# Two batches per step, K=192 as 128 plus two concurrent 64-row tiles, x transposed by DMA, and a fixed interleave of two matmul stages

## The chip, the cores and the metric

The kernel runs on one core of one Trainium2 chip. The metric is the device time of one execution in microseconds. Most executions of one kernel agree within 0.3%. Every kernel below was timed beside runs of the kernel before, on the same chip and in the same rounds. One run of all was over 1.5% above the fastest of its kernel and counts as slow; all ratios are between fast runs.

Engine names in the profile: PE is the matmul engine (TensorE), PEld its weight loads, DVE VectorE, ACT ScalarE, POOL GpSimd, SP the engine that issues most DMAs.

## The reference, cut to what matters

```python
def _attn_ref(x, weight):                 # x 8 x 4096 x 192, weight 8 heads x 7 taps
    w = softmax(weight, axis=-1)          # shortened here
    x_pad = concat([zeros(B, 6, D), x], axis=1)
    # out[b, s, head h's 24 columns] = sum over k of w[h, k] * x_pad[b, s + k, ...]

def _moe_ref(x, w_in, w_out, beta):       # x 32768 x 192, w_in 192 x 2048, w_out 2048 x 192
    h = x @ w_in
    g = h * (1.0 / (1.0 + np.exp(-beta * h)))
    return g @ w_out
```

A causal seven-tap filter over the tokens is followed by a two-layer network. Both layers together need, per 512 tokens, 16 blocks of 128 hidden features times K=192, and then K=2048 back to 192 columns.

## The kernel before

It walks through 64 tiles of 512 tokens. For each one, x is loaded with a cast to bf16, transposed on TensorE, copied out of PSUM (the memory that matmuls write to), filtered on VectorE, and multiplied twice. The 192 input features lie on two sets of 96 partitions, so every hidden block takes two matmuls of 96 rows.

```python
        x_bf = xbf_pool.tile([128, N_BLK, D], BF16)
        nc.gpsimd.dma_start(out=x_bf, in_=x_view[st])
        ptr = psum_tr.tile([128, 2 * N_BLK, BLK], BF16)
        for blk in range(N_BLK):
            nc.tensor.transpose(ptr[:DA, blk, :], x_bf[:, blk, 0:DA], ident)
            nc.tensor.transpose(ptr[:DB, N_BLK + blk, :], x_bf[:, blk, DA:D], ident)
        # ... two copies PSUM -> xt_a, xt_b; then 7 taps for a and 7 for b on VectorE -> ct_a, ct_b

        g_t = g_pool.tile([128, NF, ST_TOK], BF16)
        for pair in range(NF // 2):
            ph = psum_h.tile([128, 2, ST_TOK], FP32)
            for i in range(2):
                fc = 2 * pair + i
                nc.tensor.matmul(ph[:, i, :], w_in_sa[:DA, ts(fc, 128)], ct_a[:DA, :],
                                 start=True, stop=False)
                nc.tensor.matmul(ph[:, i, :], w_in_sb[:DB, ts(fc, 128)], ct_b[:DB, :],
                                 start=False, stop=True)
            nc.scalar.activation(g_t[:, 2 * pair : 2 * pair + 2, :], ph, AF.Silu)

        for half in range(N_BLK // 2):
            po = psum_o.tile([128, 2, D], FP32)
            for j in range(2):
                blk = 2 * half + j
                for fc in range(NF):
                    nc.tensor.matmul(po[:, j, :], g_t[:, fc, ts(blk, BLK)], w_out_s[:, fc, :],
                                     start=(fc == 0), stop=(fc == NF - 1))
            nc.vector.tensor_copy(o_sb[:, 2 * half : 2 * half + 2, :], po)
        nc.sync.dma_start(out=out_view[st], in_=o_sb)
```

The order on each engine is left to the scheduler of the framework.

## Time and profile before

| | before |
|---|---|
| median time | 1060.89 us (1060.8 to 1062.44, 3 runs) |
| TensorE busy | 85% |
| share of TensorE in the chain of waits | 78% |
| hidden matmul, start to next start, clock 1.00 | 0.2155 us |
| output matmul, start to next start | 0.0825 to 0.0865 us |
| one 512-token tile without a stall | 13.25 us |

From the page of the kernel before: busy time by engine, and busy tenths in 40 slices of the span (PEclk is the granted TensorE clock).

```profile
PE 902.9 (85%) x6656; PEld 581.1 (55%) x6656; DVE 635.5 (60%) x1313; ACT 503.7 (48%) x516; POOL 49.1 (5%) x70
PE   1699798897979979799797988979799797997968
PEclk9999899898998989899898998989989899998989
```

TensorE is nearly always busy, but with regular dips, and the clock dips with it. The groups of instructions say what the work is; the columns are line, engine, operation, tiles, shape, count, then busy time and mean duration of one, then idle time before them and what ended it.

```profile
L197 ACT ACTIVATE g_t<-ph 128x1024 bf16<-128x1024 f32 x512 | 500.5, 1021 | 540.8 <-PE ph L190 539.6
L183 PE MATMUL ph<-ct_a,w_in_sa 96*128 96x512 bf16 x1024 | 411.9, 402 | 118.7 <-DVE ct_a L171 114.3
L190 PE MATMUL ph<-ct_b,w_in_sb 96*128 96x512 bf16 x1024 | 411.0, 402 | 0.0
L205 PE MATMUL po<-w_out_s,g_t 128*128 128x192 bf16 x4096 | 386.9, 247 | 2.7
```

Durations of matmuls overlap, so a matmul's price, its *slot*, is the distance between two starts and not its mean duration: 0.2155 us, and not 0.402 us. The 114 us on the second line are TensorE waiting for the taps. The view of stretches of time shows the two regimes (columns: stretch in us, its length, busy time and count by engine, clock, DMA share, GB/s).

```profile
503.80:512.50 8.70, 1.23 (x19) 0.99 (x18) 8.70 (x17) 0.00 (x0) 2.30 (x3) 0.81 0.78 113
512.50:516.00 3.50, 3.47 (x9) 1.23 (x9) 3.50 (x11) 1.02 (x1) 0.00 (x0) 0.50 0.01 2
527.10:540.30 13.20, 13.07 (x102) 8.59 (x101) 4.57 (x10) 7.75 (x8) 0.00 (x0) 1.00 0.09 31
```

In the first stretch TensorE does almost nothing (1.23 of 8.70 us, transposes) while VectorE works without a break; in the second it is back, at half clock; in the third it is the limit at full clock.

The two matmul stages alone cost (32 x 0.2155 + 64 x 0.0845) x 64 = 787 us if every slot is full. So 273 of the 1060 us are something else: stalls, half clock, transposes, start and end.

### The profile page before, as it was taken

The page shows a single profiled execution, that of the slowest core. Times are in us where ns is not written, and L with a number is a line of the kernel's source. Part 1 is how long each engine was busy: PE and PEld are TensorE (multiplying, and loading weights), DVE is VectorE, ACT ScalarE, POOL GpSimd, SP SyncE. Part 2 cuts the span into 40 slices and gives each one's busy share as a digit, 9 for nine tenths or more (in the row PEclk, how much of TensorE's full clock was granted, in tenths as well). Part 3 has the DMA queues.
Part 4 walks back from the last instruction along what each step waited for, and adds up shares of the span by engine and source line. Part 5 has one row for each costly group of instructions (what it writes and reads, how often), then busy time and mean ns, then how long its engine had stood idle before and what let it go on. Part 6 is the DMA issues. An engine that isn't in the chain of part 4 may idle for free.

```text
span 1059.0 us, 15609 instructions
## 1 busy us (share of the span) xinstructions
PE 902.9 (85%) x6656; PEld 581.1 (55%) x6656; DVE 635.5 (60%) x1313; ACT 503.7 (48%) x516; POOL 49.1 (5%) x70
## 2 busy tenths in 40 slices
PE   1699798897979979799797988979799797997968
PEld 1366466464655646466464664646556464664645
DVE  5874564847547485464946548475474854649461
ACT  1355364453535535355353644535355352553534
POOL 2000000000000000000000000000000000000000
PEclk9999899898998989899898998989989899998989
DMA  9111312112130121301212121121201213012100
GB/s 208 12 38 38 53 32 42 32 38 38 38 54 15 38 39 38 53 16 38 41 45 44 32 43 31 38 38 38 53 16 38 38 38 53 16 38 39 37 16 31
DMA packets 72438, 42.96 MB, mean 41 GB/s; under 512 B 37232, under 2 KB 72048, under 8 KB 72048
## 3 DMA queue, kind: packets, MB, share of 16 engines
q0 software_dynamic: 33792, 12.59, 10.9%
q1 hardware_dynamic: 38576, 29.38, 8.7%
q8 instruction: 52, 0.85, 0.3%
q14 instruction: 18, 0.15, 0.0%
HBM read 29.37 MB, written 25.17 MB: 52 GB/s over the span
## 4 chain that ended last, share of the span: by engine, by line
PE 78%; DVE 13%; ACT 4%; DMA 2%; issue 1%; SPq 0%; ACTq 0%
PE po L205 33%; PE ph L183 24%; PE ph L190 21%; DVE ct_b L163 5%; DVE ct_a L163 5%; ACT g_t L197 4%; DMA beta_t<-in_moe_beta_dram 2%; DVE o_sb L212 1%; DVE ct_a L171 1%; DVE xt_b L143 1%; DVE xt_a L142 0%; DVE ct_b L159 0%; DVE ct_a L159 0%; DVE w_out_s L123 0%; SPq L78 0%
## 5 line engine op out<-in xcount | busy, mean ns | idle before, releaser
L197 ACT ACTIVATE g_t<-ph 128x1024 bf16<-128x1024 f32 x512 | 500.5, 1021 | 540.8 <-PE ph L190 539.6
L183 PE MATMUL ph<-ct_a,w_in_sa 96*128 96x512 bf16 x1024 | 411.9, 402 | 118.7 <-DVE ct_a L171 114.3
L190 PE MATMUL ph<-ct_b,w_in_sb 96*128 96x512 bf16 x1024 | 411.0, 402 | 0.0
L205 PE MATMUL po<-w_out_s,g_t 128*128 128x192 bf16 x4096 | 386.9, 247 | 2.7
L205 PEld LDWEIGHTS <-g_t 128*128 128x128 bf16 x4096 | 343.1, 98 | 71.0 <-ACT g_t L197 17.1
L212 DVE COPY o_sb<-po 128x384 f32<-128x384 f32 x128 | 71.1, 556 | 381.2 <-PE po L205 381.2
L163 DVE SCALAR_TENSOR_TENSOR ct_b<-xt_b,cw_b,ct_b 96x512 bf16<-96x512 bf16 x320 | 236.7, 740 | 0.0
L163 DVE SCALAR_TENSOR_TENSOR ct_a<-xt_a,cw_a,ct_a 96x512 bf16<-96x512 bf16 x320 | 236.6, 739 | 0.0
L190 PEld LDWEIGHTS <-w_in_sb 96*128 96x128 bf16 x1024 | 103.6, 101 | 233.2 <-issue 158.5
L183 PEld LDWEIGHTS <-w_in_sa 96*128 96x128 bf16 x1024 | 103.5, 101 | 125.8 <-issue 34.1
L133 POOL DMA_DIRECT2D x_bf<-in_x_dram x64 | 48.5, 760 | 905.1 <-PE ptr L138 903.9
L137 PE MATMUL ptr<-ident,x_bf 128*96 128x128 bf16 x256 | 39.1, 226 | 30.5 <-DMA x_bf<-in_x_dram 15.6
L137 PEld LDWEIGHTS <-x_bf 128*96 128x96 bf16 x256 | 31.0, 127 | 39.1 <-issue 17.5
L142 DVE COPY xt_a<-ptr 96x512 bf16<-96x512 bf16 x64 | 26.5, 413 | 22.4 <-PE ptr L138 22.4
L138 PE MATMUL ptr<-ident,x_bf 128*96 128x128 bf16 x256 | 38.6, 224 | 0.0
L138 PEld LDWEIGHTS <-x_bf 128*96 128x96 bf16 x256 | 31.0, 128 | 4.4
L171 DVE TENSOR_TENSOR ct_b<-xt_b,ct_b 96x512 bf16<-96x512 bf16 x64 | 26.5, 413 | 0.0
L171 DVE TENSOR_TENSOR ct_a<-xt_a,ct_a 96x512 bf16<-96x512 bf16 x64 | 26.4, 412 | 0.0
L143 DVE COPY xt_b<-ptr 96x512 bf16<-96x512 bf16 x64 | 26.2, 410 | 0.0
L159 DVE TENSOR_SCALAR ct_a<-xt_a,cw_a 96x512 bf16<-96x512 bf16 x64 | 23.0, 360 | 0.0
L159 DVE TENSOR_SCALAR ct_b<-xt_b,cw_b 96x512 bf16<-96x512 bf16 x64 | 21.8, 340 | 0.0
L150 DVE COPY xt_b<-xt_b 96x6 bf16<-96x6 bf16 x56 | 9.0, 160 | 0.0
(30 smaller groups left out, 25.8 us busy)
## 6 DMA issues: line engine op xcount, KB each, us to landing
out_dram<-o_sb SPq DMA_DIRECT2D x64, 384.0 KB
x_bf<-in_x_dram POOLq DMA_DIRECT2D x64, 192.0 KB, 5.2
w_out_t<-in_moe_w_out_dram SPq DMA_DIRECT2D x1, 1536.0 KB
beta_bc<-in_moe_beta_dram SPq DMA_DIRECT2D x1, 1024.0 KB
w_in_a<-in_moe_w_in_dram SPq DMA_DIRECT2D x1, 768.0 KB
w_in_b<-in_moe_w_in_dram SPq DMA_DIRECT2D x1, 768.0 KB
cw_a<-in_weight_dram SPq DMA_DIRECT2D x4, 0.7 KB
cw_b<-in_weight_dram SPq DMA_DIRECT2D x4, 0.7 KB
```

The source lines that it names most:

```text
L133: nc.gpsimd.dma_start(out=x_bf, in_=x_view[st])
L137: nc.tensor.transpose(ptr[:DA, blk, :], x_bf[:, blk, 0:DA], ident)
L138: nc.tensor.transpose(ptr[:DB, N_BLK + blk, :], x_bf[:, blk, DA:D], ident)
L143: nc.vector.tensor_copy(xt_b[:DB, PAD:], ptr[:DB, N_BLK : 2 * N_BLK, :])
L159: nc.vector.tensor_scalar_mul(ct[:rows, :], xt[:rows, 0:ST_TOK], cw[:rows, 0:1])
L163: nc.vector.scalar_tensor_tensor(out=ct[:rows, :], in0=xt[:rows, k : k + ST_TOK], scalar=cw[:rows, k : k + 1], in1=ct[:rows, :], op0=mybir ...
L171: nc.vector.tensor_tensor(ct[:rows, :], xt[:rows, K - 1 : K - 1 + ST_TOK], ct[:rows, :], mybir.AluOpType.add,)
L183: nc.tensor.matmul(ph[:, i, :], w_in_sa[:DA, ts(fc, 128)], ct_a[:DA, :], start=True, stop=False,)
L190: nc.tensor.matmul(ph[:, i, :], w_in_sb[:DB, ts(fc, 128)], ct_b[:DB, :], start=False, stop=True,)
L197: nc.scalar.activation(g_t[:, 2 * pair : 2 * pair + 2, :], ph, AF.Silu)
L205: nc.tensor.matmul(po[:, j, :], g_t[:, fc, ts(blk, BLK)], w_out_s[:, fc, :], start=(fc == 0), stop=(fc == NF - 1),)
L212: nc.vector.tensor_copy(o_sb[:, 2 * half : 2 * half + 2, :], po)
```

## The change: its intent and its diff

Four things at once. First, K=192 is cut as 128 + 64 in place of 96 + 96. A step takes the same 512 tokens of two batches; the 64 remaining features of one batch lie on partitions 0 to 63 and those of the other on 64 to 127, and their two 64-row matmuls are meant to run at the same time in the two halves of the array. Four slots become three. Second, x goes to DRAM as bf16 and comes back through a DMA transpose, so that TensorE transposes nothing. Third, the hidden stage of step s and the output stage of step s-1 are interleaved in a fixed order, and the taps of step s+1 are spread between them. Fourth, beta moves from the first weights into the activation's scale.

One *unit* below is one hidden block of 1024 tokens (four matmuls: two full ones, two of 64 rows) and eight output matmuls. A step has 16 units, and there are 31 full steps between the first (hidden only) and the last (output only), so 496 units.

```diff
-        x_bf = xbf_pool.tile([128, N_BLK, D], BF16)
-        nc.gpsimd.dma_start(out=x_bf, in_=x_view[st])
-        # ... TensorE transposes, copies from PSUM
+    def cast(s):
+        xd = xd_pool.tile([HALO + TOK, 3, DA], BF16, name="xd")          # DRAM
+        nc.gpsimd.dma_start(out=xd[r0:, 0:2, :], in_=x_v[p, t0:t1, :, 0:DA])
+        nc.gpsimd.dma_start(out=xd[r0:, 2, :].rearrange("t (h d) -> t h d", h=2),
+                            in_=x_v[p, t0:t1, :, DA:D])
+    def xpose(s):
+        nc.sync.dma_start_transpose(xt[:, :, r0:], xd[r0:, :, :].rearrange("t c d -> t (c d)"))
 ...
+    def hidden(s, fc):
+        ph = psum_h.tile([128, 2, TOK], FP32, name="ph")
+        w = w_in_s[:, :, fc * 128 : (fc + 1) * 128]
+        for h in range(2):
+            nc.tensor.matmul(ph[:, h, :], w[:, 0, :], ct[:, h, :], start=True, stop=False)
+        for h in range(2):
+            rows = slice(h * DB, (h + 1) * DB)                           # DB = 64
+            nc.tensor.matmul(ph[:, h, :], w[rows, 1, :], ct[rows, 2, :], start=False, stop=True)
+        nc.scalar.activation(g[:, fc, :, :], ph, AF.Silu, scale=beta[:, fc : fc + 1])
 ...
+    for s in range(N_ST + 1):
+        ops = conv_ops(s + 1) if s + 1 < N_ST else []
+        for u in range(NF):
+            if s == 0 and u % (NF // NW) == 0:
+                prep_w_in(u // (NF // NW))
+            if s < N_ST:
+                hidden(s, u)
+            if s > 0:
+                output(s - 1, u)                  # eight 128x192 matmuls, and an eviction after four
+            if u < len(ops):
+                ops[u]()                          # one tap of step s + 1
+            if s == 0:
+                prep_w_out(u)
+            if u == 0 and s + 3 < N_ST:
+                cast(s + 3)
+            if u == 1 and s + 2 < N_ST:
+                xpose(s + 2)
```

(Cut: the weights' preparation, now in four quarters, and the view of the output by batch pairs.)

## The prediction

> **What bounds it now.** The page has TensorE busy 85% and 78% of the chain of waits, ScalarE 48%, VectorE 60%. Two regimes alternate. In undisturbed 512-token tiles (the stretches 527.1 to 540.3 and 540.3 to 553.6 us) TensorE is 99% busy at granted clock 1.00 and a tile takes 13.25 us. The timeline gives its pitches: 0.2155 us for a 512-column matmul, 0.0825 to 0.0865 us for a 192-column one. So a tile is 32 x 0.2155 = 6.9 us hidden, 64 x 0.0845 = 5.4 us output, about 0.45 us of transposes, and 0.4 us of bubbles. About once in four tiles TensorE runs out, and the next two tiles' VectorE chain (copies and taps, 8.2 us) stands alone. The waits view has TensorE waiting for ct_a 114 us (16 times, about 7 us); afterwards the clock is 0.50 for 3.4 us (0.427 us pitch), 1.7 us lost each time. 64 x 13.25 = 848 us, 16 x 8.7 = 139 us more of stalls and slow clock, start 37 us and end 5 us: about 1030 of 1059.
>
> **What changes.** The K=192 product ran as two K=96 passes. It becomes one K=128 pass plus two 64-row passes of two batches at once: for 1024 tokens and 128 features 4 x 0.2155 = 0.862 us become 3 x 0.2155 = 0.646 us if the two 64-row matmuls truly overlap. The Trainium skill, "TensorEngine Tiling (Array Packing)", section "Key Properties", says such tiles run in parallel and that changing the tiling mode drains TensorE; no trace here shows either. There are two such changes per unit; I allow 0.05 us together (a guess; the array tail here, 0.377 us duration less 0.2155 us pitch, is 0.16 us, so 0.3 us is the bad case).
>
> One unit = four hidden plus eight output matmuls: 0.646 + 8 x 0.0845 + 0.05 = 1.37 us. ScalarE needs 1.03 us per unit: not the limit. VectorE per step of 16 units: taps on 128x1024 cost an estimated 1.19 us (0.66 us measured for 512, plus 512 elements at 0.96 GHz), so about 11.5 us plus four copies of 0.56 us, 13.8 us of 22: hidden, in fixed order, so the stalls and clock drops go. TensorE transposes (0.45 us a tile, 29 us) and their evictions go.
>
> Added: x through DRAM as bf16, and a DMA transpose of 528x384 a step, two steps ahead. The cast DMA becomes many rows of 256 and 128 bytes; before, 33792 packets took 10.9% of 16 engines, 55 ns each. At twice the count and perhaps twice that, about 460 us of DMA time: heavy, not limiting. The transpose, from the skill's "VectorE: DVE Perf Modes", section "The three transpose paths" (1309 ns for 128x128), is at most an estimated 16 us a step if nothing pipelines: under 22.
>
> **Sum.** Start 33 us (cast, transpose, 11 us of taps serially), step 0 limited by VectorE/ScalarE 20 us, 31 x 16 x 1.37 = 680 us, last outputs 11 us, tail 4 us: **748 us**, range **695 to 815**. Chances: faster 0.97, same 0.02, slower 0.01.
>
> **What would show it.** Right: TensorE over 95% busy with clock 1.00 in all middle slices; no long wait for ct; the pair of 64-row matmuls starting within tens of ns of each other; unit pitch about 1.37 us, step about 22 us; ScalarE about 75% busy, VectorE about 60%; transposes land in under 20 us.
> Wrong: the two 64-row matmuls 0.2155 us apart (unit 1.55 us, about 835 us); gaps of 0.1 us or more at each mode change (unit 1.5 us, 810 us); VectorE's first tap waiting each step for the DMA transpose (step over 25 us: over 850 us); a start longer than 55 us. Without any mode-change cost: about 720 us.

## The result, and the profile after

The changed kernel took 830.47 us (829.18 to 833.08, 4 runs) against 1060.85 us; the ratio of the fast runs is 0.7829, with a 95% interval of 0.7813 to 0.7845. All ratios here are the mean time of one kernel's fast runs over that of the other's of the same rounds, so they are not quite the ratio of the medians. The direction was right, but the time lies outside the predicted range of 695 to 815 us.

From the page of the kernel after, the same three lines:

```profile
PE 784.3 (95%) x6145; PEld 445.7 (54%) x6145; DVE 462.8 (56%) x613; ACT 572.7 (69%) x516; POOL 82.5 (10%) x70
PE   0279999999999999999999999999999999999997
PEclk9989999999999999999999999999999999999999
```

The dips and the slow clock are gone from the middle, as predicted. The groups:

```profile
L224 ACT ACTIVATE g<-ph,beta 128x1024 bf16<-128x1024 f32 x512 | 569.6, 1114 | 233.6 <-PE ph L221 233.6
L218 PE MATMUL ph<-ct,w_in_s 128*128 128x512 bf16 x1024 | 308.2, 383 | 31.1 <-DVE w_in_s L170 31.1
L221 PE MATMUL ph<-ct,w_in_s 64*128 64x512 bf16 x1024 | 201.7, 391 | 0.8 <-DVE w_in_s L170 0.8
L239 PE MATMUL po<-w_out_s,g 128*128 128x192 bf16 x4096 | 424.0, 247 | 0.0
```

No TensorE group shows a wait any more except for weights in the start. TensorE counts as 95% busy, and still a unit takes 1.52 us and not 1.37. The busy share cannot show this, because the recorded durations reach over the gaps. The order of time does. These are the matmuls and weight loads of one unit (start, length of the whole group, engine, line, operation, shape, count, and idle time before it):

```profile
399.78 0.59 PE L218 MATMUL ph<-ct,w_in_s 128*128 128x512 bf16 x2
400.30 0.10 PEld L221 LDWEIGHTS <-w_in_s 64*128 64x128 bf16 x2 [0.42 <-issue]
400.30 0.39 PE L221 MATMUL ph<-ct,w_in_s 64*128 64x512 bf16 x2
400.62 0.61 PEld L239 LDWEIGHTS <-g 128*128 128x128 bf16 x8 [0.23 <-issue]
400.63 0.83 PE L239 MATMUL po<-w_out_s,g 128*128 128x192 bf16 x8
401.21 0.18 PEld L218 LDWEIGHTS <-w_in_s 128*128 128x128 bf16 x2
401.30 0.59 PE L218 MATMUL ph<-ct,w_in_s 128*128 128x512 bf16 x2
```

Read the weight loads first. The load for L218 at 401.21 runs ahead of its matmul at 401.30. The load for L221 starts together with its matmul, after PEld had done nothing for 0.42 us, and so does the first load for L239: at both borders of the 64-row pair, loading ahead stops. Single starts, as the trace has them:

```
start us   took ns
399.776    379   full hidden matmul
399.992    379   full hidden matmul                       0.216 after the one before
400.304    387   64 rows, lower half                      0.312
400.307    387   64 rows, upper half                      0.003
400.626    256   output                                   0.319 after the upper half
400.719    246   output                                   0.093
400.801    246   output                                   0.082
```

The pair does overlap: 3 ns apart, and both are followed by one slot only. The Trainium skill's "TensorE: Matmul & The Clock Gate", section "The mechanism", gives about 4 ns between the starts of concurrent tiles; the trace agrees. (In e9_all_64row_pairs below, with pairs throughout, it is 20 ns.) But the distance from the last full matmul to the pair is 0.312 us where one slot is 0.2155, and from the pair to the output 0.319: about 0.10 us more at each border. The second output adds 0.01 us (0.093 where the slot is 0.0825). Together that is 0.21 us a unit: 3 x 0.2155 + 8 x 0.0825 = 1.31 us of slots, and 1.52 us measured.

The sum, term by term:

| term | predicted us | measured us | read from |
|---|---|---|---|
| until the first hidden matmul | 33 | 29.8 | timeline |
| step 0 | 20 | 31.1 | timeline, 29.8 to 60.9 |
| 496 units | 680 (1.37 each) | 754 (1.52 each) | chain of waits |
| last outputs | 11 | 10.7 | chain of waits |
| tail | 4 | 4.4 | span 829.9 |
| all | 748 | 830 | |

So 74 us of the miss of 82 us lie in the unit and 8 us in the start. For the start, the chain of waits (start, length, what):

```profile
11.05 8.90 DMA w_in_raw_107<-in_moe_w_in_dram
21.19 16.53 DMA xt<-xd
42.91 0.79 DVE w_in_s L170 x2
48.61 1.39 DVE w_in_s L170 x2
54.97 1.45 DVE w_in_s L170 x2
61.73 0.77 PE po L239 x8
```

The second transpose took 16.5 us from issue to landing (its median is 4.6 us), and each of the last three quarters of the first weights stands in VectorE's fixed order behind taps that wait for that transpose. Meanwhile GpSimd is issuing all 32 steps' casts (the DMAs that bring x to DRAM as bf16), two for each step: 35 of the 64 start in the first 63 us and the last at 102 us, because nothing makes a cast wait for its step.

```profile
POOL 8389800000000000000000000000000000000000
DMA  9999991210322221122222112222201322220111
```

### The profile page after: what moved, and what is told of

Same layout as the page of the kernel before. It is cut to its first block, busy times and chain, and to the rows that moved or that the text cites. A ratio compares the mean times of both kernels' runs of the same rounds, so it can differ in the third digit from the quotient of the medians.

```text
span 829.9 us, 13854 instructions
## 1 busy us (share of the span) xinstructions
PE 784.3 (95%) x6145; PEld 445.7 (54%) x6145; DVE 462.8 (56%) x613; ACT 572.7 (69%) x516; POOL 82.5 (10%) x70
## 3 DMA queue, kind: packets, MB, share of 16 engines
q0 software_dynamic: 68352, 12.93, 18.9%
## 4 chain that ended last, share of the span: by engine, by line
PE 93%; DMA 4%; DVE 2%; SPq 1%; issue 0%; POOL 0%; POOLq 0%
PE po L239 47%; PE ph L218 26%; PE ph L221 20%; DMA xt<-xd 2%; DMA w_in_raw_107<-in_moe_w_in_dram 1%; DVE ct L197 1%; DMA xd<-in_x_dram 1%; DVE w_out_s L177 1%; DVE w_in_s L170 0%; SPq L95 0%; SPq L133 0%; SPq L131 0%; DVE ct L195 0%; DVE ct L206 0%; SPq L136 0%
## 5 line engine op out<-in xcount | busy, mean ns | idle before, releaser
L224 ACT ACTIVATE g<-ph,beta 128x1024 bf16<-128x1024 f32 x512 | 569.6, 1114 | 233.6 <-PE ph L221 233.6
L239 PE MATMUL po<-w_out_s,g 128*128 128x192 bf16 x4096 | 424.0, 247 | 0.0
L239 PEld LDWEIGHTS <-g 128*128 128x128 bf16 x4096 | 312.4, 98 | 112.2 <-issue 112.2
L218 PE MATMUL ph<-ct,w_in_s 128*128 128x512 bf16 x1024 | 308.2, 383 | 31.1 <-DVE w_in_s L170 31.1
L197 DVE SCALAR_TENSOR_TENSOR ct<-xt,cw,ct 128x1024 bf16<-128x1024 bf16 (+1 forms) x320 | 325.1, 1016 | 8.8
L247 DVE COPY osb<-po 128x384 f32<-128x384 f32 x128 | 71.4, 557 | 329.0 <-PE po L239 329.0
L221 PE MATMUL ph<-ct,w_in_s 64*128 64x512 bf16 x1024 | 201.7, 391 | 0.8 <-DVE w_in_s L170 0.8
L221 PEld LDWEIGHTS <-w_in_s 64*128 64x128 bf16 x1024 | 49.3, 93 | 221.3 <-issue 217.8
L218 PEld LDWEIGHTS <-w_in_s 128*128 128x128 bf16 x1024 | 91.3, 98 | 36.8 <-DVE w_in_s L170 32.3
L82 POOL DMA_DIRECT2D xd<-in_x_dram x32 | 42.6, 1330 | 12.4 <-DMA xd<-in_x_dram 11.6
L83 POOL DMA_DIRECT2D xd<-in_x_dram x32 | 42.5, 1327 | 8.3 <-DMA xd<-in_x_dram 7.9
```

The lines of the kernel that those rows point to most:

```text
L82: nc.gpsimd.dma_start(out=xd[r0:, 0:2, :], in_=x_v[p, t0:t1, :, 0:DA])
L83: nc.gpsimd.dma_start(out=xd[r0:, 2, :].rearrange("t (h d) -> t h d", h=2), in_=x_v[p, t0:t1, :, DA:D],)
L197: nc.vector.scalar_tensor_tensor(out=dst, in0=src, scalar=cw[:, j, k : k + 1], in1=dst, op0=ALU.mult, op1=ALU.add,)
L218: nc.tensor.matmul(ph[:, h, :], w[:, 0, :], ct[:, h, :], start=True, stop=False)
L221: nc.tensor.matmul(ph[:, h, :], w[rows, 1, :], ct[rows, 2, :], start=False, stop=True)
L224: nc.scalar.activation(g[:, fc, :, :], ph, AF.Silu, scale=beta[:, fc : fc + 1])
```

## The experiments

**Theory A**: each change between full matmuls and 64-row matmuls costs TensorE about 0.10 us, whatever surrounds it. The tiling is paid twice per unit, and what the pair saves (one slot of 0.2155 us) goes straight back. **Theory B**: the 0.20 us come from the switch between hidden and output stage, or from the handover to ScalarE. **A second rival**: the pair does not really overlap, and its second half is what shows as gaps. Four kernels vary the number of mode changes per unit: none, one, two, four.

### e1_zero_pad: no mode change, no concurrency

```diff
+    w_in_s = consts.tile([128, 3, F], BF16)
+    nc.vector.memset(w_in_s[:, 1:3, :], 0.0)       # slot 1 + h: only the rows of batch h are filled
 ...
         for h in range(2):
-            rows = slice(h * DB, (h + 1) * DB)
             nc.tensor.matmul(
-                ph[:, h, :], w[rows, 1, :], ct[rows, 2, :], start=False, stop=True
+                ph[:, h, :], w[:, 1 + h, :], ct[:, 2, :], start=False, stop=True
             )
```

> No change of tiling mode at all: the 64-row products run as two full 128-row matmuls one after the other, the other batch's 64 weight rows set to zero. Same results. Theory A (each change of tiling mode costs TensorE about 0.10 us, 0.20 us per unit of four hidden and eight output matmuls): the unit becomes 4 x 0.2155 + 8 x 0.084 = 1.53 us against 1.52 us measured after the change, total about 836 us, so the concurrent pair is worth nothing as placed. Theory B (the 0.20 us come from switching between hidden and output matmuls, or from waits on ScalarE, and not from the mode): the 0.20 us stay and the slot of 0.2155 us is added, unit 1.74 us, total about 937 us.

Measured: 835.96 us (835.52 to 837.84, 4 runs), correct, ratio to the kernel before 0.7874 (0.7862 to 0.7885). The order of time in this run:

```profile
401.81 0.60 PE L223 MATMUL ph<-ct,w_in_s 128*128 128x512 bf16 x2
402.25 0.59 PE L225 MATMUL ph<-ct,w_in_s 128*128 128x512 bf16 x2
402.68 0.82 PE L243 MATMUL po<-w_out_s,g 128*128 128x192 bf16 x8
403.34 0.38 PE L223 MATMUL ph<-ct,w_in_s 128*128 128x512 bf16 x1
```

Each pair of hidden matmuls takes 0.43 us, two slots, and the eight output matmuls 0.66 us: no gap at any border of the stages. The unit is 1.523 us on average over a step, and its slots alone are 4 x 0.2155 + 8 x 0.0825 = 1.522. Theory B is out. As placed, the concurrent pair is worth 0.003 us a unit, 1.6 us over 496 units; of the 5.5 us between the two medians more lies in the start (first output at 64.5 us here, 61.7 in the changed kernel). The number of rows as such is not the cause either: in the kernel before, an output matmul of 128 rows starts 0.215 us after a hidden one of 96 (530.860 and 531.075), no more than a slot.

### e2_same_tile: mode changes, no concurrency

```diff
-            rows = slice(h * DB, (h + 1) * DB)
+            rows = slice(0, DB)                    # both in the lower half: wrong result
```

> Wrong result on purpose: both 64-row matmuls use rows 0 to 63, so they cannot overlap; the mode changes stay. Theory A (the pair overlaps truly, and the cost is the mode change): unit 1.52 + 0.2155 = 1.735 us, total about 937 us, and the weight load of the second one, in the same mode, is pulled ahead of its matmul. Rival (the pair does not really overlap and the 0.20 us are its second half): no change, about 830 us.

Measured: 944.89 us (944.17 to 946.06, 4 runs), the result wrong as meant, ratio 0.8897 (0.8884 to 0.891). The order of time:

```profile
402.22 0.59 PE L218 MATMUL ph<-ct,w_in_s 128*128 128x512 bf16 x2
402.74 0.11 PEld L221 LDWEIGHTS <-w_in_s 64*128 64x128 bf16 x2 [0.42 <-issue]
402.75 0.60 PE L221 MATMUL ph<-ct,w_in_s 64*128 64x512 bf16 x2
```

The unit is 1.733 us. Taking the overlap away costs one slot, so the overlap was real. In this run the two weight loads of 64 rows were issued together (0.11 us for both, their matmuls 0.227 us apart) though both go to the same rows: being 64-row does not stop loading ahead, changing to it does.

### e3_four_changes: full, 64, full, 64

```diff
         for h in range(2):
             nc.tensor.matmul(ph[:, h, :], w[:, 0, :], ct[:, h, :], start=True, stop=False)
-        for h in range(2):
             rows = slice(h * DB, (h + 1) * DB)
```

> Order full, 64-row, full, 64-row, so four mode changes a unit and no concurrency; same results. Theory A: 4 x 0.2155 + 8 x 0.084 + 4 x 0.102 = 1.94 us a unit, total about 830 + 496 x 0.42 = 1038 us. Theory B (no cost per mode change): only the lost overlap, 1.735 us, about 937 us.

Measured: 1068.18 us median (1058.45 to 1123.22, 4 runs, of which the last, 1123.22, counts as slow), correct; ratio of the fast runs to the kernel before 1.0026 (0.9978 to 1.0074). The order of time:

```profile
402.14 0.38 PE L218 MATMUL ph<-ct,w_in_s 128*128 128x512 bf16 x1
402.45 0.39 PE L220 MATMUL ph<-ct,w_in_s 64*128 64x512 bf16 x1
402.77 0.39 PE L218 MATMUL ph<-ct,w_in_s 128*128 128x512 bf16 x1
403.10 0.39 PE L220 MATMUL ph<-ct,w_in_s 64*128 64x512 bf16 x1
403.42 0.84 PE L238 MATMUL po<-w_out_s,g 128*128 128x192 bf16 x8
```

Every border, of either kind, is 0.31 to 0.32 us where a slot is 0.2155. The unit is 1.94 us, as Theory A says. The total is 30 us over its 1038: the first output comes 9 us later than in the changed kernel, and the 12 units after it ran at half pace, 3.44 us each (18 us more). The chain of waits of this run shows the pace changing (an output group takes 1.40 us before 112 us and 0.77 after); what held it at half pace is open:

```profile
108.71 1.40 PE po L238 x8
112.15 0.77 PE po L238 x8
```

### e4_group2: one mode change per unit

```diff
+        for fc, ph in zip(fcs, phs):               # fcs: two neighbouring units
+            for h in range(2):
+                nc.tensor.matmul(ph[:, h, :], w, ct[:, h, :], start=True, stop=False)
+        for fc, ph in zip(fcs, phs):
+            for h in range(2):
+                rows = slice(h * DB, (h + 1) * DB)
+                nc.tensor.matmul(ph[:, h, :], w, ct[rows, 2, :], start=False, stop=True)
 ...
-                hidden(s, u)
+                if u % 2 == 0: hidden_group(s, (u, u + 1))
```

(Shortened: w is the unit's slice of the first weights, and the activations follow in a loop of their own.)

> Two units grouped: four full hidden matmuls, then four 64-row ones, then sixteen output matmuls, so two mode changes per two units. Same results. Theory A: unit 1.317 + 0.102 = 1.42 us, total about 830 - 496 x 0.10 = 780 us. Theory B (the cost follows the hidden/output switches or the ScalarE handover): the number of hidden/output switches also halves, so it may gain as well, but then run e1_zero_pad must show 1.74 us. If the three hidden buffers are too few for groups of two, waits for ScalarE will show before the full hidden matmuls and the gain is smaller.

Measured: 777.33 us (775.18 to 780.17, 4 runs), correct, ratio 0.7311 (0.7297 to 0.7326).

```profile
401.45 1.03 PE L219 MATMUL ph<-ct,w_in_s 128*128 128x512 bf16 x4
402.41 0.61 PE L224 MATMUL ph<-ct,w_in_s 64*128 64x512 bf16 x4
402.95 1.49 PE L243 MATMUL po<-w_out_s,g 128*128 128x192 bf16 x16
404.28 1.03 PE L219 MATMUL ph<-ct,w_in_s 128*128 128x512 bf16 x4
```

Two units in 2.83 us; on average over a step 1.413 us each.

The four together: 0, 1, 2 and 4 changes per unit. After the slots are taken off (4, 3, 3 and 4 hidden slots of 0.2155 us and 8 x 0.0825 us), 0.00, 0.11, 0.21 and 0.42 us are left: 0.105 to 0.107 us for each change.

What happens in that time? The trace narrows it down. The last full matmul of the unit above starts at 399.992, so one slot later, near 400.207, the next could have started; the first load in the new mode starts only at 400.299, 0.092 us later (at the other border it is 0.100 us). The load itself then adds little: its matmul follows 0.005 us later, and the first two output matmuls are 0.093 us apart in place of 0.0825. The same 0.01 us shows in the kernel before, where a load of g_t waited for ScalarE and was not ahead (starts 549.878 and 549.970, 0.092 us). So of each change 0.09 to 0.10 us is a wait before the first load and about 0.01 us the load. That the wait is the array emptying is what the Trainium skill's "TensorEngine Tiling (Array Packing)", section "Key Properties", says ("drains the TensorE"); the trace shows only the wait, not what fills it.

### The start: e5_gate_casts and e6_prep_first

```diff
+    def gate(ap):
+        nc.gpsimd.tensor_copy(gate_sb, ap)         # one element; GpSimd waits for it
 ...
             if u == 0 and s + 3 < N_ST:
+                gate(cts[s][0:1, 2, 0:1])
                 cast(s + 3)
```

> Only the start is touched: from the fourth step on, each step's cast of x waits until the taps of three steps before are done (a one-element copy on GpSimd), so the casts no longer all run in the first 63 us. Theory A (the second transpose, 16.5 us from issue to landing in the start against 4.6 us in the median, is late because all the casts compete for the DMA engines): it lands about 10 us earlier, step 1 starts near 51 us instead of 61.7, total about 820 us. Rival (the start is held by VectorE's fixed order, weights behind taps, and by the weight loads): unchanged within 3 us. The later steps must keep their 1.52 us per unit: nothing there waits for a cast.

(The 63 us in this text is a misreading: as said above, the casts' issue lasts until 104 us.)

Measured: 819.22 us (818.9 to 819.38, 4 runs), correct, ratio 0.7715 (0.7704 to 0.7727). The chain of waits:

```profile
19.64 10.07 DMA xt<-xd
49.26 0.77 PE po L244 x8
```

The second transpose landed at 29.7 us and not at 37.7, and the first output came at 49.2 and not at 61.7 us. The units kept their 1.52 us.

```diff
     for op in conv_ops(0):
         op()
+    for i in range(NW):
+        prep_w_in(i)                               # before the taps of step 1, no longer between them
 ...
-            if s == 0 and u % (NF // NW) == 0:
-                prep_w_in(u // (NF // NW))
```

> Only VectorE's order is touched: all four quarters of the first weight matrix are prepared before the taps of step 1. Theory A (casts): TensorE then runs step 0 without its 7.5 us wait for weights, but step 1 still waits for the late transpose plus 17 us of VectorE work, so about 6 us gained, 824 us. Rival (VectorE's order is what matters): the whole 12 us, about 818 us.

Measured: 826.54 us (825.75 to 827.86, 4 runs), correct, ratio 0.7786 (0.7774 to 0.7798). The gain is 4 us, a little less than either theory had said; the first output came at 55.8 us, but TensorE still ran the first two units at half pace. So holding back the casts (11.3 us) gains more of the long start than VectorE's order (3.9 us).

### Versions built on it: e7_group2_start and e8_group3_nobeta

e7 joins the groups of two and both changes of the start, and loads half of the first weights before the first transpose (diffs here and below shortened to what matters).

```diff
     cast(0)
+    cast(1)
+    # loads of w_in, quarters 0 and 1
 ...
     xpose(0)
+    # loads of w_in, quarters 2 and 3
 ...
-    cast(1)
+    gate(xts[0][0:1, 0, HALO : HALO + 1])
     cast(2)
     xpose(1)
+    # load of w_out
 ...
+    prep_w_in(0)
+    prep_w_in(1)
     for op in conv_ops(0):
         op()
+    for i in range(2, NW):
+        prep_w_in(i)
```

> Groups of two units plus both changes of the start, and half of the first weight matrix loaded before the first transpose. If the two gains are independent: 777 us of the groups alone less 12 to 14 us, about 764 us.

Measured: 764.67 us (763.96 to 765.22, 4 runs), correct, ratio 0.72 (0.7188 to 0.7212). The groups and the changed start add: 12.7 us less than the groups alone. The two changes of the start do not add in full, since alone they gave 11.3 and 3.9 us.

```diff
-            if s < N_ST and u % 2 == 0: hidden_group(s, (u, u + 1))
+            n = {0: 3, 3: 3, 6: 3, 9: 3, 12: 2, 14: 2}.get(u, 0) if s else 1
+            if s < N_ST and n: hidden_group(s, range(u, u + n))
 ...
-            nc.scalar.activation(g[:, fc, :, :], ph, AF.Silu, scale=beta[:, fc : fc + 1])
+            nc.scalar.activation(g[:, fc, :, :], ph, AF.Silu)      # beta in w_in_s again
```

> As the run before, but groups of three (four threes and two twos in a step, so 6 times 2 mode changes per 16 units) and beta folded into the first weights again, so that the activation takes no scale per partition. Theory A: unit 1.317 + 0.204 x 6/16 = 1.39 us, about 496 x 0.026 = 13 us less than groups of two: about 751 us. ScalarE's activation should go back from 1.11 to 1.02 us; if it stays at 1.11, three buffers do not cover a group of three and TensorE waits for ScalarE before the third unit (an estimated 1.43 us a unit, about 770 us).

Measured: 752.82 us (751.49 to 753.4, 4 runs), correct, ratio 0.7089 (0.7078 to 0.7099). The unit is 1.387 us on average over a step. Two things were changed here, so the 12 us are not divided between them. ScalarE:

```profile
L249 ACT ACTIVATE g<-ph 128x1024 bf16<-128x1024 f32 x512 | 489.2, 1025 | 231.6 <-PE ph L245 231.6
```

1025 ns in place of 1114: the scale per partition had cost 0.09 us of each activation. In the changed kernel that time was off the critical path.

### e9_all_64row_pairs: no mode change and full overlap

If only the change costs, then it is enough never to change. Cut everything into 64 rows.

```diff
+        for j in range(3):                         # 192 = 3 x 64 rows, one batch in each half
+            for h in range(2):
+                rows = slice(h * DB, (h + 1) * DB)
+                nc.tensor.matmul(ph[:, h, :], w_in_s[rows, j, fc * 128 : (fc + 1) * 128],
+                                 ct[rows, j, :], start=(j == 0), stop=(j == 2))
 ...
+            for t in range(2):                     # output: the two halves of 128 rows, two banks
+                rows = slice(t * DB, (t + 1) * DB)
+                nc.tensor.matmul(po[:, t, q % 2 * D : (q % 2 + 1) * D],
+                                 g[rows, fc, h, q * BLK : (q + 1) * BLK], w_out_s[rows, fc, :],
+                                 start=(fc == 0), stop=(fc == NF - 1))
 ...
+            nc.vector.tensor_copy(dst, po[:, 0, 0 : 2 * D])
+            nc.vector.tensor_tensor(dst, po[:, 1, 0 : 2 * D], dst, ALU.add)
```

(Cut: x, its taps and the first weights laid out in three slices of 64 features, both halves of the partitions alike. ph has two buffers in place of three, because po now takes two banks.) Here each half keeps to its own bank.

> No mode change at all and yet full overlap: every matmul, hidden and output, is cut into 64-row pieces that run in pairs, one in rows 0 to 63 and one in rows 64 to 127, each pair writing two PSUM banks. The hidden layer takes 192 = 3 x 64 rows, one batch in each half of the array; the output's two halves of 128 rows are added by VectorE at eviction. Start as in e8_group3_nobeta. Same results, 22 matmuls and 22 weight loads per unit instead of 12. Theory A (only the mode change costs; pairs overlap fully, as one hidden pair did): unit 3 x 0.2155 + 8 x 0.0835 = 1.315 us, 496 x 0.075 = 37 us less than e8_group3_nobeta, about 718 us (a start some 3 us longer). Rival (the overlap holds for one long pair, but the issue of twice as many instructions, or the weight loads of two tiles, limits a stream of short pairs): hidden pairs still 0.2155 us apart, but output pairs over 0.10 us apart, unit above 1.45 us, slower than e8_group3_nobeta.

Measured: 724.58 us (724.07 to 725.17, 4 runs), correct, ratio 0.6822 (0.6811 to 0.6833). The order of time and the groups:

```profile
400.58 0.83 PE L243 MATMUL ph<-ct,w_in_s 64*128 64x512 bf16 x6
401.22 0.84 PE L267 MATMUL po<-w_out_s,g 64*128 64x192 bf16 x16
401.88 0.83 PE L243 MATMUL ph<-ct,w_in_s 64*128 64x512 bf16 x6
```

```profile
L243 PE MATMUL ph<-ct,w_in_s 64*128 64x512 bf16 x3072 | 426.6, 378 | 23.1 <-DVE ct L230 21.0
L267 PE MATMUL po<-w_out_s,g 64*128 64x192 bf16 x8192 | 428.3, 243 | 0.0
L267 PEld LDWEIGHTS <-g 64*128 64x128 bf16 x8192 | 370.0, 94 | 101.1 <-issue 0.5
```

A unit is 1.307 us: six hidden matmuls in the time of three and sixteen output ones in the time of eight, without a gap. Almost none of the output loads' idle time is "issue" any more. Twice as many instructions did not limit it: in the output stage the two of a pair start 20 ns apart, and the next pair 63 ns later. VectorE pays for it with a second operation at each eviction. The total is 7 us over the expected 718, mostly for the start: its first output came at 57.0 us (49.9 in e8_group3_nobeta), and the first units again ran at half pace. It has 21 shorter taps, 14 loads of small weights and three casts a step; which of these lengthens the start was not tried.

| kernel | median us | ratio to before | mode changes per unit | unit us (most steps) | first output us |
|---|---|---|---|---|---|
| the change | 830.47 | 0.7829 | 2 | 1.520 | 61.7 |
| e1_zero_pad | 835.96 | 0.7874 | 0 | 1.523 | 64.5 |
| e2_same_tile (wrong result) | 944.89 | 0.8897 | 2 | 1.733 | 69.4 |
| e3_four_changes | 1068.18 | 1.0026 (0.9978 to 1.0074) | 4 | 1.942 | 70.8 |
| e4_group2 | 777.33 | 0.7311 | 1 | 1.413 | 63.8 |
| e5_gate_casts | 819.22 | 0.7715 | 2 | 1.520 | 49.2 |
| e6_prep_first | 826.54 | 0.7786 | 2 | 1.520 | 55.8 |
| e7_group2_start | 764.67 | 0.72 | 1 | 1.413 | 48.8 |
| e8_group3_nobeta | 752.82 | 0.7089 | 0.75 | 1.387 | 49.9 |
| e9_all_64row_pairs | 724.58 | 0.6822 | 0 | 1.307 | 57.0 |

## Why the prediction was right or wrong, point by point

- **The stalls and the slow clock go: right.** TensorE waits for no tap after the start, and the clock stays at its full grant in the middle slices. Together with the transposes this is where the gain comes from: with the 787 us of matmul slots taken off, 273 us were left before and 49 us in e1_zero_pad, which has the same slots as before and none of the packing. The packing itself brought 5.5 us at most, 1.6 of them in the units. No run separates what ended the stalls: the fixed order, or a VectorE with less to do (462.8 us busy, 635.5 before).
- **The step that failed: "There are two such changes per unit; I allow 0.05 us together (a guess ...)".** They cost 0.21 us together, 0.105 to 0.107 each, as the runs with 0, 1, 2 and 4 changes show. The change was named as a cost, and its term was four times too small: with output slots of 0.0825 us, where 0.0845 was assumed, the unit was 0.15 us too long, 496 x 0.15 = 74 us. The prediction had a figure at hand, the tail of 0.16 us by which a matmul's recorded duration exceeds its slot; 0.105 us is nearer to that than to 0.025, and the two changes lie below its "bad case" of 0.3. Its list of signs had "gaps of 0.1 us or more at each mode change (unit 1.5 us, 810 us)", and that came true; the start (8 us) and a unit of 1.52 us make the rest of the way to 830.
- **The pair overlaps truly: right.** Starts 3 ns apart, and taking it away (e2) cost 114 us, one slot per unit and a slower start.
- **Start: 53 us, measured 61.** The first hidden matmul came earlier than predicted (29.8, not 33), but step 0 took 31 us, not 20. The prediction counted the casts' DMA time but not when they run; nothing held them back, and they were all issued in the first 104 us. Gating them gave back 11 us.
- **The casts' DMA time: wrong, without effect on the units.** Predicted about 460 us of the 16 engines' time; the page has 18.9% of 830 us, 157 us, with 68352 packets, twice as many as before but 37 ns each and not 110.
- **The DMA transpose: right that it hides.** Median 4.6 us from issue to landing for 528x384, against the estimate of at most 16 us. No first tap waits for it after the start.
- **ScalarE at 1.03 us: wrong, without effect.** It was 1.11 us, since the scale became a value per partition. The Trainium skill's "ScalarE: Activation LUTs", section "What ACT_TABLE_LOAD costs", gives about 93 ns for each such operand, and 1114 less 1021 ns is just that; the prediction had not looked it up.
- **VectorE: right.** A tap on 128x1024 took 1.19 us in the chain of the start, as estimated, and about 1.32 us from start to start in the middle of the run; VectorE was 56% busy, for 60 predicted.

## What to carry to other kernels

Before packing small matmuls into parts of the array, count how often the stream changes between full and partial tiles: here each change cost 0.105 us, half of the 0.2155 us slot that the pair saves, so two changes around one pair leave nothing, while groups of pairs, or a stream that is cut into equal pieces throughout, keep the gain. The busy share cannot show this loss; look in the order of time for a weight load that starts together with its matmul and not ahead of it. And a prefetch that nothing holds back runs at once: with fixed order on every engine, gate it, or it competes with the loads that the start is waiting for.

## What the Trainium skill lacked or had wrong

- "TensorEngine Tiling (Array Packing)", section "Key Properties", says that a change of tiling mode drains TensorE but gives no figure. The runs: 0.105 to 0.107 us per change at full clock, much the same from full to 64 rows and back, of which about 0.01 us is the weight load. At half pace, in step 0 of the changed kernel, it was about the same, 0.115 us (two full matmuls and the change 0.97 us, pair and change 0.54 us, with slots of 0.427 us): the slot doubled and the change did not. Neither the page nor any trace here says what fills it.
- The same page does not say that a whole kernel can be cut into 64-row pairs at no loss of TensorE time. Here 22 matmuls and 22 weight loads ran in 1.307 us, the slots of 11 full ones.
- "TensorE: Matmul & The Clock Gate", section "Back-to-back issue gap", gives a sustained 131 ns for N=512 in a stream of loads and matmuls. The full matmuls of the runs here show 215.5 ns, close to its figure for the single gap.
- The same page, Part 1, has the clock released after one busy window of about 3.4 us. In e3_four_changes TensorE counted as 31.05 of 32 us busy from 80 to 112 us and still ran at half pace (an output group of 1.40 us, 0.77 later), with a granted clock of 1.00 in the records. The counted durations reach over the gaps at the mode changes, so TensorE was less busy than counted, and the run does not show the page wrong. Why it lasted 41 us is open.
- "VectorE: DVE Perf Modes", section "The three transpose paths", has 1309 ns for one 128x128 DMA transpose and no larger size. Here 528x384, 12.4 times as much, landed in a median of 4.6 us, an estimated 0.37 us per 128x128.
